# A cold beginning on one core: row numbers by iota in place of a load, two table scalings moved up, and a label for a branch hint at the end

## The chip, the cores and the metric

The kernel runs on 1 core of one Trainium2 chip. Times are microseconds of the device for one whole execution. Executions of the same program scatter by 3 to 4 us here (0.2%).

Engines: PE is the TensorE matmul engine (PEld its weight loads), DVE is VectorE, ACT is ScalarE, POOL is GpSimd, SP is SyncE, which issues most DMAs. A q behind an engine's name in a profile line (SPq, POOLq) stands for its sequencer, which waits, branches and issues DMAs.

## The reference, cut to what matters

```python
def _A_ref(x, w_r, w_i):
    X = rfft2(x.astype(float32)) * (w_r + 1j * w_i)
    return irfft2(X, s=(S, D)).astype(bfloat16)
# _B_ref: attention over 64 segments of 32 rows, 32 heads of 128, with 8 memory rows
#         that each segment hands to the next, and a projection by Wo   (cut)
x = A_x                                   # [1, 2048, 640], bf16
x = x + _A_ref(_layernorm(x), A_w_r, A_w_i)
x = x + _B_ref(_layernorm(x), B_mem0, B_Wq, B_Wk, B_Wv, B_Wo, B_seg_len)
x = x + _A_ref(_layernorm(x), A_w_r, A_w_i)
x = x + _B_ref(_layernorm(x), B_mem0, B_Wq, B_Wk, B_Wv, B_Wo, B_seg_len)
return x
```

## The kernel before

The first A layer starts cold: nothing is in SBUF yet. Row tiles of x (16 tiles of 128 rows) arrive in five loads. The layernorm is not applied to x; instead each row tile's scale is multiplied into its 128x128 Fourier table ("scaled tables"), and the mean is subtracted by extra matmuls ("means"). The stage goes in five groups of row tiles. For each group: statistics on DVE (ACT takes three of the tiles), a *small chain* that makes the scales, the scaled tables on DVE, the matmuls on PE into PSUM tiles, and the evictions of those tiles by ACT or DVE.

```python
def cold_raw(self, x_src, s3):
    ...                                                       # cut
    for a, b in ((0, 2), (2, 4), (4, 8), (8, 12), (12, 16)):
        nc.sync.dma_start(out=x[:, a:b, :], in_=r16(x_src)[:, a:b, :])
        ...                                                   # tables of a >= 4
    groups = [(0, 4), (4, 8), (8, 12), (12, 14), (14, 16)]
    pp = tc.alloc_tile_pool(name=f"{self.lname}_ps1", bufs=8, space=PSUM)   # 8 buffers, the "banks" below

    def scales(q):                                            # the small chain
        small = nc.gpsimd if q < 4 else nc.vector             # L289
        nc.scalar.activation(... func=ACTF.Ln ...)            # ACT first, L290
        nc.scalar.activation(... func=ACTF.Exp, scale=-0.5)   # L291
        ...                                                   # then seven or so ops on `small`
    def stats(t):                                             # L310, L311: bn_stats x2, bn_aggr on DVE
    def scale_tables(q):
        for t in range(*groups[q]):                           # L315
            nc.vector.tensor_scalar_mul(out=Ts[:, t, :], in0=T[:, t, :], scalar1=rs[:, t:t + 1])
    def matmuls(q):                                           # L324 rows, L329 means; five PSUM tiles
    def empties(q, ps, by):                                   # L262; one letter per PSUM tile
        ...                                                   # "A": ACT evicts it, "D": DVE
    with tc.manual_schedule(engines={PE, ACT, DVE, POOL}):    # the order below is each engine's order
        ...
        ps2 = matmuls(2)
        stats(14)
        stats(15)
        scales(4)
        empties(1, ps1, "  AAA")
        scale_tables(3)
        ps3 = matmuls(3)
        scale_tables(4)
        empties(2, ps2, "AAADD")
        empties(3, ps3, "AADAD")
        ps4 = matmuls(4)
        empties(4, ps4, "DADAD")
```

The A layer also needs rows of its weights in mirrored order. POOL gathers them with two indirect DMAs, whose row numbers 127..0 lie in a small table, itself loaded at the start by POOL's own DMA queue:

```python
def load_mirror(self, i):                                     # L220, twice in cold_raw
    nc.gpsimd.indirect_dma_start(out=self.Wm[:, i, :], in_=..., in_offset=IndirectOffsetOnAxis(ap=g["mirror"][:, 0:1], axis=0), ...)

nc.gpsimd.dma_start(out=g["mirror"][:], in_=nc.inline_tensor(np.arange(127, -1, -1, ...)).ap())   # L1595
```

The end: the last B layer adds its projection to x and stores each row tile. Then a flag decides whether a slow general version must redo the work. With this data it never does; the branch at L1676 jumps over it to the end of the program.

```python
def run(self, ...):                                           # _FastOut
    for t in range(16):
        for k in (2 * t, 2 * t + 1):
            ps = first[k] if k < len(first) else psx()
            self.accumulate(ps, k, lhs, ...)                  # 32 matmuls, L1393
            nc.vector.tensor_tensor(out=x[...], in0=ps[:, 0:320], in1=x[...], op=ALU.add)   # L1404
        if nxt is None:
            nc.sync.dma_start(out=self.xd[:, t, :], in_=x[:, t, :])                         # L1406
...
cond = nc.values_load(fa[0:1, 0:1], min_val=0, max_val=1)
with tc.If(cond > 0):                                         # L1676
    general_B(...)                                            # not taken
```

## Time and profile before

The median of 3 runs is 1582.58 us (1579.89 to 1582.95). The profiled execution took 1580.74 us by the same clock; its trace has a span of 1578.9 us, and all times of the trace below are counted in that span.

| milestone of the profiled execution | us |
|---|---|
| DVE starts statistics of row tile 4 ("row 4") | 8.57 |
| first matmul on PE | 10.88 |
| PE steps to full clock (first clock record) | 14.48 |
| first matmul of stage 2 ("S2") | 27.32 |
| first matmul of the first B layer's loop | 134.51 |
| last add starts | 1572.10 |
| SP at its branch, and its next instruction | 1573.00, 1575.55 |
| DVE at its branch, and its next instruction | 1572.73, 1575.99 |
| last output landed | 1574.71 |
| end of the span | 1578.90 |

The page of the kernel before gives the span, the busy time of each engine, and PE's busy tenths in 40 slices:

```profile
span 1578.9 us, 36639 instructions
PE 1542.9 (98%) x14420; PEld 1074.0 (68%) x14421; DVE 784.2 (50%) x2198; ACT 835.6 (53%) x2549; POOL 280.3 (18%) x327
...
PE   6999999999999999999999999999999999999998
```

Only the first slice of 39 us and the last show PE busy for less than 90%, and those are the two places that the change touches.

The timeline of the kernel before (start and duration in us, engine, line, operation, output <- inputs, count; in brackets the idle time before it and what ended it):

```profile
1.24 0.76 POOL L1595 DMA_DIRECT2D mirror<-mirror_tbl  x1 [0.78 <-POOLq L1701]
...
8.57 0.89 DVE L310 BATCH_NORM_STATS2 A1xn_S<-A1x_S 128x6 f32<-128x320 bf16 x2 [1.59 <-DMA A1x_S<-in_A_x_dram]
...
10.61 0.70 DVE L315 TENSOR_SCALAR A1xn_S<-A1xn_S 128x128 bf16<-128x128 bf16 x4
10.88 1.61 PE L324 MATMUL ps<-A1xn_S,A1x_S 128*128 128x128 bf16 x12 [10.88 <-DVE A1xn_S L311]
12.28 1.06 PE L329 MATMUL ps<-A1xn_S 128*128 128x128 bf16 x8
...
16.68 0.61 PE L329 MATMUL ps<-A1xn_S 128*128 128x128 bf16 x8
...
21.74 0.16 DVE L301 SCALAR_TENSOR_TENSOR A1xn_S<-A1xn_S 128x2 f32<-128x2 f32 x1 [0.40 <-ACT A1xn_S L291]
22.69 0.74 DVE L315 TENSOR_SCALAR A1xn_S<-A1xn_S 128x128 bf16<-128x128 bf16 x4
23.08 0.51 PE L324 MATMUL ps<-A1xn_S,A1x_S 128*128 128x128 bf16 x6 [0.21 <-DVE A1xn_S L315]
24.18 0.27 PE L324 MATMUL ps<-A1xn_S,A1x_S 128*128 128x128 bf16 x2
...
27.32 0.86 PE L424 MATMUL ab<-A1tab_S,A1YT_S 128*128 128x321 bf16 x5 [0.52 <-DVE A1YT_S L262]
```

POOL issues its small load at 1.24. DVE stood idle for 1.59 us at 8.57, until row tiles 4 to 7 of x had landed; PE's first matmul at 10.88 follows the first scaled tables, begun at 10.61. The last small chain has DVE waiting 0.40 us for ACT at 21.74, and the tables of rows 12-13 come only behind it, at 22.69; PE waits 0.21 us for them at 23.08.

Between 4 and 5 us the DMA engines are busy for 0.79 of the time and yet move only 72 GB/s: their packets are slow, not absent.

At the end, SP's own waits of the kernel before (who waited, for what: total us, times, longest):

```profile
SPq L1676 <- SPq L1676: 2.5, 1, 2.5
```

SP waits 2.5 us on itself at the branch, and the span ends 6.80 us after the last add began.

### The profile page before, as it was taken

What the parts mean: (1) busy time and instruction counts of PE and PEld (TensorE: products, weight loads), DVE (VectorE), ACT (ScalarE), POOL (GpSimd) and SP (SyncE); (2) the same over time, 40 slices, a digit from 0 to 9 for tenths busy, and PEclk for the clock granted to TensorE, in tenths of its full rate; (3) what the DMA queues carried; (4) which work ended last, traced back from release to release, by engine and by line L of the source; (5) the groups of instructions that cost most, each with busy time, mean ns of one, the idle gap of its engine ahead of it and who ended that gap; (6) DMA issues with size and microseconds to landing.
All of it is one profiled execution on the core that took longest, in us unless ns stands there. A gap on an engine that the chain in (4) does not pass through costs nothing. (4 is left out here: it accounts for less than half of the span.)

```text
span 1578.9 us, 36639 instructions
## 1 busy us (share of the span) xinstructions
PE 1542.9 (98%) x14420; PEld 1074.0 (68%) x14421; DVE 784.2 (50%) x2198; ACT 835.6 (53%) x2549; POOL 280.3 (18%) x327
## 2 busy tenths in 40 slices
PE   6999999999999999999999999999999999999998
PEld 5676666666766666677766766666766666677775
DVE  7972545455454545533377535454554545543101
ACT  4484666666666666511126656666666666663000
POOL 3620111121211112100034101111212111120000
PEclk9999999999999999999999999999999999999999
DMA  4680445445444453636114514445454454437242
GB/s 167 207 303 14 141 130 138 145 117 173 128 142 128 123 174 99 213 101 182 51 49 150 186 54 138 133 120 175 123 149 122 134 162 130 141 97 227 68 129 62
DMA packets 159922, 214.13 MB, mean 136 GB/s; under 512 B 7230, under 2 KB 133500, under 8 KB 151804
## 3 DMA queue, kind: packets, MB, share of 16 engines
q1 hardware_dynamic: 159132, 209.41, 44.7%
q8 instruction: 114, 1.87, 0.5%
q0 software_dynamic: 608, 2.30, 0.4%
q14 instruction: 68, 0.56, 0.1%
HBM read 166.59 MB, written 45.09 MB: 134 GB/s over the span
## 5 line engine op out<-in xcount | busy, mean ns | idle before, releaser
L1087 PEld LDWEIGHTS <-bB_S 128*128 128x128 bf16 x3180 | 258.0, 97 | 174.7 <-issue 1.1
L1237 DVE TENSOR_TENSOR bB_S<-pso,bB_S 128x480 bf16<-128x480 f32 (+1 forms) x320 | 189.6, 593 | 246.6 <-PE pso L1228 235.5
L1166 ACT ACTIVATE bB_S<-pss 128x269 bf16<-128x269 f32 (+5 forms) x576 | 204.1, 386 | 198.8 <-PE pss L1163 193.6
L1393 PE MATMUL psx<-Wo_sb,bB_S 128*128 128x320 bf16 x2048 | 287.7, 299 | 0.0
L1146 DVE CAST bB_S<-psk 128x495 bf16<-128x495 f32 (+3 forms) x320 | 191.8, 600 | 114.0 <-PE psk L1087 75.8
L1393 PEld LDWEIGHTS <-bB_S 128*128 128x128 bf16 x2048 | 197.1, 98 | 74.3 <-DVE bB_S L1237 0.7
L1167 DVE TENSOR_TENSOR bB_S<-bB_S,maskf 128x269 bf16<-128x269 bf16 (+5 forms) x576 | 159.6, 289 | 162.1 <-ACT bB_S L1166 162.1
L1192 POOL TENSOR_TENSOR bB_S<-bB_S,bB_S 128x634 f32<-128x634 f32 x62 | 95.1, 1534 | 682.1 <-ACT bB_S L1187 682.1
L1155 ACT CAST bB_S<-psv 128x512 bf16<-128x512 f32 (+1 forms) x288 | 161.5, 561 | 75.4 <-PE psv L1153 74.8
L1131 ACT ACTIVATE bB_S<-psq 128x96 bf16<-128x96 f32 x300 | 152.8, 509 | 91.1 <-PE psq L1087 90.2
L1153 PE MATMUL psv<-bB_S,B1hT_S 128*128 128x256 bf16 x1360 | 166.2, 273 | 0.0
L1153 PE MATMUL psv<-bB_S,B2hT_S 128*128 128x256 bf16 x1360 | 166.2, 273 | 0.0
L1087 PE MATMUL psk<-B1hT_S,bB_S 128*128 128x495 bf16 (+3 forms) x800 | 162.4, 343 | 0.4 <-ACT bB_S L1108 0.2
L1087 PE MATMUL psk<-B2hT_S,bB_S 128*128 128x495 bf16 (+3 forms) x800 | 162.4, 343 | 0.3 <-ACT bB_S L1108 0.2
L1163 PEld LDWEIGHTS <-bB_S 128*128 128x128 bf16 x1216 | 99.6, 97 | 84.4
L1087 PE MATMUL psq<-B1hT_S,bB_S 128*128 128x495 bf16 (+5 forms) x780 | 153.2, 336 | 0.0
L1087 PE MATMUL psq<-B2hT_S,bB_S 128*128 128x495 bf16 (+5 forms) x780 | 153.2, 336 | 0.0
L1153 PEld LDWEIGHTS <-B2hT_S 128*128 128x128 bf16 x1360 | 127.5, 98 | 14.6 <-issue 0.2
L1153 PEld LDWEIGHTS <-B1hT_S 128*128 128x128 bf16 x1360 | 127.5, 98 | 14.6 <-issue 0.2
L1163 PE MATMUL pss<-bB_S 128*128 128x132 bf16 (+8 forms) x1216 | 133.0, 215 | 0.1
L1228 PE MATMUL pso<-bB_S,bB_S 128*128 128x132 bf16 (+8 forms) x1216 | 120.2, 216 | 1.5 <-DVE oTmf L1238 1.4
L1228 PEld LDWEIGHTS <-bB_S 128*128 128x128 bf16 x1216 | 90.6, 98 | 22.8 <-DVE oTmf L1238 4.0
(282 smaller groups left out, 1541.8 us busy)
## 6 DMA issues: line engine op xcount, KB each, us to landing
bB_S<-Rd SPq DMA_DIRECT2D x62, 1059.5 KB
oTx_d<-bB_S SPq DMA_DIRECT2D x60, 512.0 KB
bB_S<-oTx_d SPq DMA_DIRECT2D x46, 512.0 KB
bB_S<-in_B_Wq_dram SPq DMA_DIRECT2D x32, 320.0 KB
bB_S<-in_B_Wk_dram SPq DMA_DIRECT2D x32, 320.0 KB
bB_S<-in_B_Wv_dram SPq DMA_DIRECT2D x32, 320.0 KB
Wo_sb<-in_B_Wo_dram SPq DMA_DIRECT2D x4, 1280.0 KB
B1wv_S<-in_B_Wv_dram SPq DMA_DIRECT2D x10, 512.0 KB
```

Source lines behind the costliest of these rows:

```text
L1087: nc.tensor.matmul(ps, lhsT=w[:, ch, hh * 128:(hh + 1) * 128], rhs=src[:, ch, lo:hi], start=(ch == 0), stop=(ch == 4))
L1131: nc.scalar.mul(out=qv[:, :, 0:SEG], in_=x_view(ps, o, n)[:, :, 1:SW], mul=scale)
L1146: nc.vector.tensor_copy(out=KTs[h % 2][:, lo:hi], in_=ps[:, 0:hi - lo])
L1153: nc.tensor.matmul(ps[:, i * 256:(i + 1) * 256], lhsT=hT[:, ch, st.hcol((t + i) * 128):st.hcol((t + i) * 128) + 128], rhs=w["Wv"][:, ch, : ...
L1155: nc.scalar.copy(out=V[:, t:t + n, :].rearrange("p a b -> p (a b)"), in_=ps[:, 0:n * 256])
L1163: nc.tensor.matmul(ps[:, off - o0:off - o0 + hi - lo], lhsT=KT[:, t * 128:(t + 1) * 128], rhs=QT[:, lo:hi], start=True, stop=True)
L1166: nc.scalar.activation(out=E[:, 0:n], in_=ps[:, 0:n], func=ACTF.Exp)
L1167: nc.vector.tensor_tensor(out=P[:, o0:o0 + n], in0=E[:, 0:n], in1=bs.mask[:, o0:o0 + n], op=ALU.mult)
L1192: nc.gpsimd.tensor_tensor(out=accS, in0=accS, in1=sums_sb, op=ALU.add)
L1228: nc.tensor.matmul(pso[:, lo - q0:hi - q0], lhsT=V[:, t, (h % 2) * 128:(h % 2 + 1) * 128], rhs=P[:, off:off + hi - lo], start=(i == 0), st ...
L1237: nc.vector.tensor_tensor(out=oT.rearrange("p (r s j) -> p r s j", r=16, j=2)[:, :, s0:s0 + ns, :], in0=byclass(po), in1=rx, op=ALU.mult)
L1393: self.tc.nc.tensor.matmul(ps[:, 0:320], lhsT=lhs(h, k // 2), rhs=self.g["Wo_sb"][:, h, c0:c0 + 320], start=(h == 0), stop=(h == H - 1))
```

## The change

The intent is to shorten both ends. At the cold beginning, POOL makes the row numbers itself (iota) and no longer loads them. DVE scales the tables of rows 12-13 while it would wait for ACT in the last small chain. At the end, a hint is to tell the engines about the coming branch.

```diff
@@ cold_raw
             stats(14)
             stats(15)
+            scale_tables(3)
             scales(4)
             empties(1, ps1, "  AAA")
-            scale_tables(3)
             ps3 = matmuls(3)
@@ _FastOut.run
                 ps = first[k] if k < len(first) else psx()
+                if nxt is None and k == 31:
+                    self.tc.mark_branch_hint_location("general")
                 self.accumulate(ps, k, lhs, n_first if k < len(first) else 0, H)
@@ make_globals
-    nc.gpsimd.dma_start(out=g["mirror"][:], in_=nc.inline_tensor(np.arange(127, -1, -1, dtype=np.int32).reshape(128, 1), name="mirror_tbl").ap())
+    nc.gpsimd.iota(g["mirror"][:], pattern=[[0, 1]], base=127, channel_multiplier=-1)
@@ end
-    with tc.If(cond > 0):
+    with tc.If(cond > 0, label="general"):
```

In the built programs, the instruction counts differ by one iota more and one DMA less, and nothing else. The mark emitted no hint instruction: a mark that names no engines emits none.

## The prediction

> **What bounds the kernel now.** The page has PE busy for 98% of a 1578.9 us span; only the first slice shows less (6 tenths). The change touches the first 27 us and the last 7 us.
>
> *Beginning (timeline).* PE starts at 10.88 us. The chain before it: rows 4-7 of x land, DVE statistics of row 4 start at 8.57 (1.59 us idle, ended by the DMA of x), scaled tables at 10.61, first matmul. From 8.57 to 27.3 DVE has almost no gap; stage 2 starts on PE at 27.31, released by DVE's last eviction.
>
> *End (instruction records, SP's own waits).* The last DVE add ends at 1572.59; its output lands at 1574.7. SP branches at 1573.0 and goes on only at 1575.55 (2.5 us of SP waiting on itself, with 8 and 16 KB instruction packets in that time). [...] A working hint could save at most the 0.85 us by which it outlasts the landing.
>
> **What the change does.**
>
> 1. *Iota for the load.* Removes a 0.76 us issue on POOL and a 4.4 us transfer (landed at 5.66), needed only by the mirrored gathers at 9.63 and 14.99, so its latency gates nothing. But in the packet records the first packet of rows 4-7 on each DMA engine, right behind that engine's 4-byte write of this load, takes 0.4 to 2.2 us instead of 0.196, and the data rate drops at 4.5-6 us. If the load causes that hole, rows 4-7 come up to 1 us earlier; if it is only that transfer's own start, nothing is gained. I give that one half. As built, POOL's identity memset and select (0.23, 0.29 us) move into the first small chain, which then ends near 9.6 instead of 9.06; DVE's statistics hide that. So 0 to 1.0 us, expected 0.4.
>
> 2. *Tables of rows 12-13 earlier.* Two multiplies (about 0.37 us) fill the 0.40 us in which DVE waits for ACT's exp (21.34-21.74). DVE gains 0.35 us and PE's 0.21 us wait at 23.08 goes. But the later PSUM tiles of rows 12-13 reuse banks that ACT frees until about 24.1 (PE takes the last at 24.18), and ACT's order is unchanged. So 0 to 0.2 us, about 0.1.
>
> 3. *Branch hint.* The built program has no new hint: instruction counts differ by one iota and one DMA only, and all ten prefetch hints are in the fallback's loops, as before. Gain 0.
>
> **Predicted.** About 0.5 us less: 1581.3 us, 8 in 10 between 1578.8 and 1583.2. The spread of before (1579.89 to 1582.95) exceeds the effect. Faster by over 2%: 0.005; within 2%: 0.99; slower by over 2%: 0.005.
>
> **What would show each step.** (1) DVE's statistics of row 4 move from 8.57 toward 7.6 and PE's first matmul from 10.88 toward 9.9; or both stay. (2) Table scaling ahead of the 21.7 us step, PE's idle at 23.08 gone, PE still waiting for ACT at the last tile. Stage 2 starts at 26.3 to 27.2. (3) SP's wait at the branch stays 2.5 us and the span ends 6.3 us after the last add.
>
> **What would make it wrong.** A hint that works after all (0.85 us more); an iota slow to start that delays the first small chain past 10.6 us; a table of stage 2 made late by the shifted DMAs.

## More of the kernel before

The stretches view of the kernel before (window, length, busy time and count of each engine, granted clock of PE, mean busy share of the DMA engines, GB/s). The last line is one stretch of 4 us far from the change:

```profile
core 0: us, PE busy (x) PEld busy (x) DVE busy (x) ACT busy (x) POOL busy (x), PEclk, DMA share, GB/s
4.00:5.00 1.00, 0.00 (x0) 0.00 (x0) 0.96 (x4) 0.32 (x1) 0.00 (x0) 1.00 0.79 72
5.00:6.00 1.00, 0.00 (x0) 0.00 (x0) 0.97 (x4) 0.97 (x3) 0.00 (x0) 1.00 0.71 220
72.00:76.00 4.00, 3.00 (x15) 2.08 (x15) 2.88 (x4) 1.57 (x6) 1.06 (x1) 0.57 0.67 229
```

## The result, and the profile after

The kernel after takes 1579.57 us (median of 6 runs, 1578.48 to 1581.57); before, now with 6 runs, 1580.60 us (1579.89 to 1582.95). The ratio is 0.9991 [0.9979, 1.0004]: the same within 2%, and at the edge of what can be told from no difference.

The profiled executions differ by more, 1578.9 against 1577.2 us. The page after, where every engine's busy time is nearly unchanged (PE 1541.9 against 1542.9 us):

```profile
span 1577.2 us, 36639 instructions
PE 1541.9 (98%) x14420; PEld 1073.3 (68%) x14421; DVE 783.7 (50%) x2198; ACT 834.3 (53%) x2549; POOL 279.3 (18%) x327
```

The timeline of the kernel after (its line numbers are two higher from L1402 on):

```profile
0.87 0.12 POOL L1597 IOTA mirror<- 128x1 int32 x1 [0.41 <-POOLq L1703]
...
7.69 0.89 DVE L310 BATCH_NORM_STATS2 A1xn_S<-A1x_S 128x6 f32<-128x320 bf16 x2 [0.75 <-DMA A1x_S<-in_A_x_dram]
...
10.04 1.60 PE L324 MATMUL ps<-A1xn_S,A1x_S 128*128 128x128 bf16 x12 [10.04 <-DVE A1xn_S L315]
...
20.18 0.36 DVE L315 TENSOR_SCALAR A1xn_S<-A1xn_S 128x128 bf16<-128x128 bf16 x2
20.86 0.16 DVE L301 SCALAR_TENSOR_TENSOR A1xn_S<-A1xn_S 128x2 f32<-128x2 f32 x1 [0.24 <-ACT A1xn_S L291]
21.67 0.45 PE L324 MATMUL ps<-A1xn_S,A1x_S 128*128 128x128 bf16 x4
22.33 0.27 PE L324 MATMUL ps<-A1xn_S,A1x_S 128*128 128x128 bf16 x2 [0.21 <-ACT A1YT_S L262]
...
23.30 0.27 PE L324 MATMUL ps<-A1xn_S,A1x_S 128*128 128x128 bf16 x2
...
26.44 1.82 PE L424 MATMUL ab<-A1tab_S,A1YT_S 128*128 128x321 bf16 x12 [0.52 <-DVE A1YT_S L262]
```

DVE's wait for x is 0.75 us instead of 1.59, so row 4 starts 0.88 us earlier; PE's first matmul is 0.84 us earlier (10.04) and S2 0.88 us. The iota that replaces the load took 0.12 us. From row 4 to S2 it is 18.75 us in both kernels. So the moved tables gained nothing, though they did move (20.18, ahead of the step at 20.86), and PE did begin rows 12-13 0.53 us earlier when counted from row 4 (21.67 - 7.69 = 13.98 against 23.08 - 8.57 = 14.51). PE then stands still for ACT at 22.33, which has not yet evicted a bank. The last tile of those rows starts 15.61 us after row 4 in both (23.30 - 7.69 and 24.18 - 8.57).

The stretches of the kernel after:

```profile
4.00:5.00 1.00, 0.00 (x0) 0.00 (x0) 0.97 (x4) 0.38 (x1) 0.00 (x0) 1.00 1.06 415
5.00:6.00 1.00, 0.00 (x0) 0.00 (x0) 0.96 (x4) 0.97 (x3) 0.00 (x0) 1.00 0.91 339
72.00:76.00 4.00, 3.47 (x27) 2.58 (x28) 2.75 (x5) 2.86 (x10) 0.17 (x1) 1.00 0.43 146
```

The hole at 4 to 5 us is gone: 415 GB/s against 72. SP's own wait at the branch has not changed:

```profile
SPq L1678 <- SPq L1678: 2.5, 1, 2.5
```

Where the 1.67 us between the two profiled executions (1578.90 to 1577.23) come from:

| stretch | before | after | difference |
|---|---|---|---|
| start to S2 | 27.32 | 26.44 | -0.88 |
| S2 to the first B layer's loop | 107.19 | 106.35 | -0.84 |
| loop to last add | 1437.59 | 1437.73 | +0.14 |
| last add to end | 6.80 | 6.71 | -0.09 |

The second line is not the change's. In the execution of before, PE was granted half clock for one window of 3.413 us at 72.50 (the stretch 72 to 76 above: clock 0.57, 15 matmuls started against 27); in that of after it was not (clock 1.00). Both have such a window near 847 us. In both executions PE works through the same lull there, waiting for POOL and ACT. Counted over windows of 3.413 us laid out from the clock records, PE was busy for 1.75 of the 3.41 us just before 72.50 in before, and for 1.82 and 2.13 us in the two windows that cover the lull in after. All windows of the two lulls (near 72 and 846 us) with less than 2.2 us of work, over all fourteen profiles, give the same split: the 24 with 1.13 to 1.75 us were each followed by a half-clock window, and the 7 with 1.82 to 2.16 us were not. (The boundary is no sharper than that: in e12 the window in which the kernel's work ends, with 1.74 us, was not followed by one.) And the three profiles without a half-clock window near 72 us (after, e8, e11) took 106.33 to 106.38 us from S2 to the loop, the eleven with one 107.18 to 107.82. So half of what the two traces show is this one half-clock window, and only 0.88 us are left for the change to explain, less than the scatter between executions.

### The clock in these traces

In these traces the clock changes on a grid: every half-clock window inside the work is 3.413 us long, and in before the step to full clock at 14.48 and the window at 72.50 lie 58.02 us apart, 17 windows. The other stretches of full clock in the clock records, 771.41 and 723.63 us in before and 832.85 and 723.63 us in after, are 226, 212, 244 and 212 windows long. The step has no fixed distance from the first matmul: in the eleven profiles of unwarmed kernels it came 2.86 to 5.77 us after it. This is a lottery that every comparison of single executions has to take out. It can be taken out: on the first ten profiles I fitted

S2 = the later of (row 4 + 18.72) and ((first matmul + clock step) / 2 + 14.03).

The first is DVE's chain. The second is PE's: up to the step PE does about half the work (a matmul every 107 ns, later every 56, in before), so that its 14.03 us of full-speed work ends when the formula says. It holds within 0.05 us for nine of the ten (0.12 for the tenth, e8), and it gave 26.77 for e9, which was not in the fit and measured 26.77. Before and after lie on the first branch; an execution with a late step lies on the second, and then the earlier x gains less.

### The profile page after: what moved, and what is told of

Same layout as the page of the kernel before. It is cut to its first block, busy times and chain, and to the rows that moved or that the text cites. A ratio compares the mean times of both kernels' runs of the same rounds, so it can differ in the third digit from the quotient of the medians. Undisturbed runs are those within 1.5% of the kernel's fastest.

```text
span 1577.2 us, 36639 instructions
## 1 busy us (share of the span) xinstructions
PE 1541.9 (98%) x14420; PEld 1073.3 (68%) x14421; DVE 783.7 (50%) x2198; ACT 834.3 (53%) x2549; POOL 279.3 (18%) x327
```

## The experiments

All twelve kernels gave the right result. Each timed one ran 5 times beside 9 runs of before on the same chip; e9 was a single look.

| run | what it is | median us | ratio to before [95%] | row 4 | clock step | S2 | last add to end |
|---|---|---|---|---|---|---|---|
| before | | 1580.60 | | 8.57 | 14.48 | 27.32 | 6.80 |
| after | | 1579.57 | 0.9991 [0.9979, 1.0004] | 7.69 | 13.22 | 26.44 | 6.71 |
| e1 | iota alone | 1579.87 | 0.9991 [0.9978, 1.0005] | 7.81 | 15.88 | 27.01 | 7.19 |
| e2 | tables alone | 1580.80 | 0.9998 [0.9985, 1.0012] | 8.52 | 15.30 | 27.25 | 6.66 |
| e3 | marks alone | 1581.12 | 1.0003 [0.9989, 1.0016] | 7.72 | 13.98 | 26.42 | 7.14 |
| e4 | after, plus the load, unread | 1580.48 | 0.9996 [0.9982, 1.0010] | 8.81 | 16.34 | 27.76 | 6.77 |
| e5 | real hints just before the end | 1580.87 | 1.0001 [0.9988, 1.0015] | 7.13 | 15.07 | 26.41 | 7.07 |
| e6 | real hints at the start | 1578.91 | 0.9987 [0.9974, 1.0001] | 8.39 | 15.91 | 27.37 | 4.81 |
| e7 | evictions first | 1580.49 | 0.9997 [0.9984, 1.0011] | 7.87 | 15.98 | 27.11 | 6.77 |
| e8 | the load from ACT's queue | 1580.63 | 1.0001 [0.9988, 1.0015] | 7.57 | 12.80 | 26.41 | 6.55 |
| e9 | hints in between (one run) | 1579.75 | | 8.00 | 15.19 | 26.77 | 5.86 |
| e10 | e6, PE warmed | 1577.66 | 0.9983 [0.9970, 0.9997] | 7.22 | 6.43 | 26.08 | 4.81 |
| e11 | e10, evictions first | 1577.79 | 0.9977 [0.9964, 0.9991] | 8.36 | 6.35 | 26.37 | 4.97 |
| e12 | e11, tables not moved | 1578.95 | 0.9986 [0.9973, 1.0000] | 7.98 | 5.03 | 26.71 | 4.79 |

### The three parts alone: e1, e2, e3

My theory: the load made the hole, so the iota carries all the gain; the tables and the marks carry none. The rival: the tables carry it and the hole is the transfer's own beginning.

e1 is before with the iota line alone.

```diff
-    nc.gpsimd.dma_start(out=g["mirror"][:], in_=nc.inline_tensor(...).ap())
+    nc.gpsimd.iota(g["mirror"][:], pattern=[[0, 1]], base=127, channel_multiplier=-1)
```

> Only the row numbers come from iota; table order and the end are as before. Theory (the load stalled the x packets of rows 4-7): all of the gain at the beginning is here: DVE's statistics of row 4 at 7.6 to 7.8 us (before 8.57, after 7.69), PE's first matmul near 10.0, stage 2's first matmul at 26.4 to 26.5. Rival (the earlier table scaling, not the load, made stage 2 start earlier): row 4 at 8.5, stage 2 at 27.2 to 27.4. Total about 0.9 us below before, give or take the clock windows.

Row 4 came at 7.81, very near what was expected, but S2 only at 27.01, against 26.4 to 26.5. The reason is the clock: the step came at 15.88. The timeline of e1:

```profile
27.01 1.27 PE L424 MATMUL ab<-A1tab_S,A1YT_S 128*128 128x321 bf16 x8 [0.52 <-DVE A1YT_S L262]
```

From row 4 to S2 it is 19.20 us here instead of 18.75: PE, not DVE, was the slower. This miss is what led to the formula above.

e2 is before with the tables moved alone.

```diff
+            scale_tables(3)
             scales(4)
             empties(1, ps1, "  AAA")
-            scale_tables(3)
```

> Only the tables of rows 12-13 are scaled earlier. Theory: ACT's freeing of the PSUM banks paces PE here, so PE's idle before the first matmul of rows 12-13 goes, but stage 2 starts at 27.2 to 27.35 us, at most 0.1 us earlier than before (27.32). Rival: DVE paces it, and the 0.35 us that DVE gains arrive at stage 2, near 26.97. Total within 0.2 us of before but for the clock windows.

The timeline of e2:

```profile
23.07 0.50 PE L324 MATMUL ps<-A1xn_S,A1x_S 128*128 128x128 bf16 x6
...
24.12 0.27 PE L324 MATMUL ps<-A1xn_S,A1x_S 128*128 128x128 bf16 x2
...
27.25 1.00 PE L424 MATMUL ab<-A1tab_S,A1YT_S 128*128 128x321 bf16 x6 [0.52 <-DVE A1YT_S L262]
```

PE's wait for the tables is gone from the line at 23.07, but the last tile starts at 24.12, 15.60 us after row 4, and S2 is 18.73 us after it. The tables alone are worth nothing.

e3 is before with the two lines of the hint alone.

```diff
+                if nxt is None and k == 31:
+                    self.tc.mark_branch_hint_location("general")
-    with tc.If(cond > 0):
+    with tc.If(cond > 0, label="general"):
```

> Only the mark and the label. The built program is the same as before, instruction for instruction, so this run measures what the same program scatters by. Theory: stage 2 at 27.3 plus or minus 0.1, SP idle 2.5 us after its branch, end 6.7 to 6.9 us after the start of the last add; any difference of the total from before is scatter, with a step of 0.8 to 1.0 us for each half-clock window of TensorE that one execution has and the other has not. Rival (the mark does something that the instruction list doesn't show): SP's idle falls below 1.7 us.

The built program has the same instructions as before. Its row 4 came at 7.72, as early as in the kernels without the load. Its timeline and its stretch:

```profile
7.72 0.89 DVE L310 BATCH_NORM_STATS2 A1xn_S<-A1x_S 128x6 f32<-128x320 bf16 x2 [0.61 <-DMA A1x_S<-in_A_x_dram]
```

```profile
4.00:5.00 1.00, 0.00 (x0) 0.11 (x1) 0.97 (x3) 0.23 (x1) 0.00 (x0) 1.00 0.77 90
```

The hole at 4 to 5 us is there as in before (90 GB/s), and still row 4 is early. One execution's row 4 proves nothing about the load; the packets do. Of them, more at e4. SP's wait at the branch is 2.9 us here, so the marks do nothing. S2 at 26.42, against the 27.3 expected, and the end 7.14 us after the last add, against 6.7 to 6.9, are misses: the same program scatters by more than I had allowed.

### Is it the load? e4 and e8

e4 puts the load back beside the iota, into a tile that nobody reads. If the load's traffic costs the time, it must come back.

```diff
     nc.gpsimd.iota(g["mirror"][:], pattern=[[0, 1]], base=127, channel_multiplier=-1)
+    g["mirror_d"] = sp.tile([128, 1], I32, name="mirror_d")
+    nc.gpsimd.dma_start(out=g["mirror_d"][:], in_=nc.inline_tensor(...).ap())
```

> After, with the old load put back on POOL's queue into a tile that nobody reads. Theory (the load's traffic does it): row 4's statistics go back to 8.4 to 8.6 us and stage 2 to 27.2 to 27.4, though nothing waits for the load. Rival (what counts is that the gathers no longer wait for the load, or that POOL's order changed): row 4 stays at 7.7 and stage 2 at 26.4.

Row 4 came at 8.81 and S2 at 27.76, even later than expected (S2 in part because the clock step came as late as 16.34). In the stretches of e4, the rate at 4 to 6 us is about half of what it is without the load:

```profile
4.00:5.00 1.00, 0.00 (x0) 0.00 (x0) 0.96 (x4) 0.45 (x1) 0.00 (x0) 1.00 0.91 205
5.00:6.00 1.00, 0.00 (x0) 0.00 (x0) 0.97 (x4) 0.97 (x3) 0.00 (x0) 1.00 0.63 200
```

e8 keeps the load but issues it from ACT and not from POOL, whose queue the page of before calls software_dynamic (32 packets from 3 to 7 us in before, none in after).

```diff
-    nc.gpsimd.dma_start(out=g["mirror"][:], in_=nc.inline_tensor(...).ap())
+    nc.scalar.dma_start(out=g["mirror"][:], in_=nc.inline_tensor(...).ap())
```

> Before, with the same load of 128 times 4 bytes issued from ACT in place of POOL at nearly the same time. Theory (POOL's software path stalls the DMA engines): the first 128 packets of rows 4-7 take 1 to 3 us more than 0.196 each in sum, as in the two runs without the load (1.7 and 1.4), 13 of 16 landings by 6.3 us, row 4's statistics at 7.2 to 7.8. Rival (any load of many tiny rows does it): 8 to 12 us in sum, 13 of 16 landings after 7.2.

The stretches of e8:

```profile
4.00:5.00 1.00, 0.00 (x0) 0.10 (x1) 0.58 (x2) 0.00 (x0) 0.00 (x0) 1.00 1.09 382
5.00:6.00 1.00, 0.00 (x0) 0.00 (x0) 0.97 (x4) 0.76 (x2) 0.00 (x0) 1.00 0.99 394
```

No hole. The bytes of the load are the same, but two things differ: the queue, and the time. ACT issues the load at 0.79 (POOL did at 1.24), and it has landed by 4.16, before the first packet of rows 4-7 starts at 4.60; in before it landed from 4.32 to 5.66, among those packets. So e8 does not show which of the two matters, the queue or the coincidence in time. The expectation that x would land as without the load failed, because the load now stands ahead of x: the first rows of x landed at 4.39 us instead of about 3.8. Its time, 1580.63 us, shows no gain over before.

The decisive measure is in the packet records of the trace. The first 128 packets of rows 4 to 7 have 5120 bytes each and take 0.196 us when undisturbed. What they took beyond that, summed, and the landing of the 13th and the last of the 16 DMA engines' shares of these rows:

| | sum of excess, us | 13th landing | last landing |
|---|---|---|---|
| with POOL's load: before, e2, e3, e4 | 12.4, 8.4, 9.5, 11.8 | 7.55, 7.58, 7.22, 7.27 | 8.48, 8.42, 7.62, 8.71 |
| without: after, e1, e5, e6, e7, e9, e10, e11, e12 | 1.7, 1.4, 1.0, 2.2, 2.9, 2.6, 0.8, 4.0, 4.5 | 6.15, 6.28, 6.24, 6.35, 6.33, 6.15, 6.28, 6.34, 6.39 | 7.59, 7.71, 6.37, 8.29, 7.77, 7.90, 6.41, 8.26, 7.88 |
| load from ACT: e8 | 2.4 | 6.99 | 7.09 |

The two groups do not overlap in the first two columns. In before, most slow packets are the ones right behind a 32-byte row and a 4-byte write of POOL's load (4.2 to 5.3 us; single packets of 0.99, 1.35, 1.49 and 2.17 us). The records do not name the engine; the pairing is by time: 14 packets of rows 4-7 start within 12 ns of the end of such a write, and they took 0.28 to 2.17 us. In e4 it is otherwise: 4.3 of its 11.8 us lie in packets that began before the load's first write (4.56 us), so being right behind the write is not the whole mechanism. What stretches x's packets next to the load, to as much as 2.17 us, is not in the records.

The last column shows why row 4 scatters all the same. DVE starts right behind the last share (landed at 8.48, start 8.57 us in before; 7.59 and 7.69 in after), and in seven of the nine profiles without POOL's load the last landed 1.43 to 1.94 us behind the 13th, in the other two 0.13. The packet records here do not name the engine, so the cause of these late shares stays open. Over all profiles, row 4 starts at 8.41 us on average with POOL's load (four) and at 7.83 without (nine): 0.58 us. But the two groups overlap (7.72 to 8.81 and 7.13 to 8.39), so for row 4 itself the difference is likely and not proven; it is the packets that the load changes without overlap.

### The hint: e5, e6, e9

With `engines=` given, a mark emits real hint instructions. e5 puts them behind the last work of row tile 14: 3 instructions ahead of the branch on SP, 4 on DVE, and about 138 on PE, counted in the trace.

```diff
+                if t == 14:
+                    for ins, e in ((mm, nc.tensor), (add, nc.vector), (dma, nc.sync)):
+                        with self.tc.issue_after(ins.ins):
+                            self.tc.mark_branch_hint_location("general", engines=[e.engine])
```

> After, with the mark made to emit: engines are named (PE, DVE, SP), and each hint stands behind that engine's work for row 14, some 5 to 8 us before the end. Theory (the 2.5 to 3 us after the branch are a fetch that a real hint can start earlier): SP's idle after its branch falls from 2.5-3.0 us to below 1.7 us and is then ended by the landing of the last output; span end minus start of the last add falls from 6.7-7.2 us to 5.7-6.2. Rival (the idle is the wait for the output's landing, or the fetch starts only at the branch): both stay. Beginning as in after: excess of the first 128 packets of rows 4-7 below 3 us.

For SP and DVE that theory failed. SP's own wait in e5, and likewise DVE's 3.3 us from branch to next instruction, stayed:

```profile
SPq L1681 <- SPq L1681: 2.7, 1, 2.7
```

PE's hint worked, which does not show at the end because PE is done before the others: its branch instruction took 0.41 us, against 3.35 to 3.77 us in the nine profiles where PE has no hint, after among them, and a 16 KB instruction packet starts 1.2 us behind the hint (1561.86 and 1560.63), where after has none. DVE's and SP's hints were as early in time, 9.3 and 8.7 us ahead of their branches. So it is not the time that they lacked.

e6 takes the change's own mark and only adds the engines. The built program then has the hint as the first instruction of all five engines, since nothing ties it to a place.

```diff
-                    self.tc.mark_branch_hint_location("general")
+                    self.tc.mark_branch_hint_location("general", engines=list(mybir.ALL_ENGINES))
```

> After, with the changed kernel's own mark at its own place, and all five engines named. The build puts the five hints at the very start of the program, whole milliseconds of instructions ahead of the branch. Theory A (a hint is held until its branch): same end as with the late hints. Theory B (it only fetches at once[...]): end as in after, 6.7 to 7.2 us behind the start of the last add; up to 0.3 us later start.

SP went on 0.53 us after its branch and DVE 0.61 us (2.55 and 3.26 in before). SP's own waits in e6:

```profile
SPq L1678 <- SPq L1678: 0.9, 2, 0.5
```

The span ended 4.81 us after the last add instead of 6.80; over all profiles it is 4.79 to 4.97 us with hints at the start (four) and 6.55 to 7.19 with no hint or hints just before the end (nine). Neither of the two theories had this: late hints and hints at the start do not end alike, and the early hint's effect was not gone after 1570 us. In the timed runs, e6 is at a mean of 1578.90 us beside 1580.85 for its before.

e9 separates distance from presence: SP's hint some 490 instructions before its branch, DVE's 47 before.

```diff
+                        with tc.issue_after(dma.ins):           # SP, in the first B layer
+                            tc.mark_branch_hint_location("general", engines=[nc.sync.engine])
+            if nxt is None and t == 0:                          # DVE, in the last B layer's output loop
+                with self.tc.issue_after(add.ins):
+                    self.tc.mark_branch_hint_location("general", engines=[nc.vector.engine])
```

> After, with hints on two engines alone at two distances: SP's some 490 of its instructions ahead of its branch (behind a load at the end of the first B layer), DVE's 47 ahead (behind the first add of the last stage). The hints 3 and 4 instructions ahead did nothing, those at the program's start did. Theory [...]: SP's idle after the branch is below 0.7 us as with hints at the start, DVE's stays at 3.2 to 3.4 us. Rival (only a hint at the head of the program works): both stay (SP 2.5 to 3.1). Second rival (3 or 4 instructions were just too few): both fall. Span end minus start of the last add: between 4.8 and 7.1, set by the slower engine.

SP's branch took 0.53 us and DVE's 3.27 us, in one and the same execution. SP's waits of e9, none of which at the branch is longer than 0.7 us:

```profile
SPq L1681 <- SPq L1681: 1.2, 2, 0.7
...
SPq L1720 <- DVEq L1681: 1.0, 1, 1.0
```

The second line is the point: once SP's branch is quick, SP waits 1.0 us for DVE at the end. Both engines must be hinted; e9's tail of 5.86 us lies between 6.80 and 4.81. A hint worked 494 instructions ahead of its branch (SP) and about 138 (PE in e5), and not 47, 4 or 3 ahead (DVE in e9, DVE and SP in e5). But these are different engines and the exact limit was not tried, so the least distance, and why the distance counts, stay open. e9's single run has an unknown state; its reading rests on the waits of two engines in the same execution, not on its time.

### Why the moved tables gave nothing: e7, e10, e11, e12

The reading of after was that ACT frees the banks too late. ACT's order has the last small chain's two operations ahead of the evictions of rows 4-7's tiles. e7 turns that around.

```diff
+            empties(1, ps1, "  AAA")
             scale_tables(3)
             scales(4)
-            empties(1, ps1, "  AAA")
             ps3 = matmuls(3)
```

> After, with ACT's three evictions of rows 4-7's last tiles ahead of the last small chain, in the 1.2 us in which ACT waits for DVE there. Theory (ACT's freeing of PSUM banks paces PE in rows 12-15): row 4's statistics to stage 2 takes 18.2 to 18.4 us in place of 18.70 to 18.75, and PE no longer waits inside rows 12-13. Rival (PE's work or DVE's evictions pace it): 18.65 to 18.8. A late step of TensorE to full clock (after 15 us) can add 0.4 us to either.

Inconclusive: the clock step came at 15.98, PE was busy without a gap from 17.3 to 26.6 us, and S2 was 19.24 us after row 4 as the second branch of the formula has it. Nothing that helps DVE or ACT can show while PE is behind. So the clock had to be taken out. e10 is e6 with 84 matmuls on data that is there early, written to a PSUM tile that nobody reads, so that PE's clock step comes before the work.

```diff
+            warm = pp.tile([128, 4, 128], FP32, name="warm", tag="pa")
+            for n, w in ((32, g["ones"][:]), (28, x[:, 2, 0:128]), (24, x[:, 4, 0:128])):
+                for i in range(n):
+                    nc.tensor.matmul(warm[:, i % 4, :], lhsT=w, rhs=g["ones"][:], start=True, stop=True)
             act_stats(3)
```

> After, with hints on all engines at the program's start and 84 matmuls of no use on PE before the first real one (their result is never read), so that TensorE's step to full clock comes early. From ten profiles: stage 2 starts at the later of row 4's statistics + 18.72 us and half of (PE's first real matmul + step) + 14.03 us, within 0.1. Theory (that law): the step comes before 9.5 us, and stage 2 starts 18.65 to 18.85 us after row 4's statistics. Rival (the extra 0.3 to 0.5 us of four runs had another cause): 18.9 to 19.3. End 4.7 to 5.0 us behind the start of the last add. Total 0 to 0.5 us below the run with the hints at the start (1578.91).

The timeline of e10:

```profile
1.24 3.59 PE L347 MATMUL warm<-ones 128*128 128x128 bf16 x32 [1.24 <-DVE ones L1608]
...
10.78 0.61 PE L329 MATMUL ps<-A1xn_S 128*128 128x128 bf16 x8
...
22.12 0.27 PE L324 MATMUL ps<-A1xn_S,A1x_S 128*128 128x128 bf16 x2 [0.21 <-ACT A1YT_S L262]
...
26.08 2.10 PE L428 MATMUL ab<-A1tab_S,A1YT_S 128*128 128x321 bf16 x14 [0.52 <-DVE A1YT_S L262]
```

The first real means-matmuls take 0.61 us already, the clock step is at 6.43, and PE still waits for ACT at 22.12, with S2 18.86 us after row 4. That is a hair above the 18.65 to 18.85 expected, and below the rival's 18.9 to 19.3. The hair has a likely reason: row 4 came so early (7.22) that DVE's first tables (9.44) start right behind POOL's last multiplication of the scales (9.21 to 9.41), 2.22 us after row 4 against 2.04 in before. By this trace an x that lands earlier still would gain little, though no run tried it. A warm PE alone does not shorten DVE's chain; it only removes the late branch. The median, 1577.66 us, is 1.25 us below e6's, more than the 0 to 0.5 expected, but on another chip. e11 adds e7's order.

```diff
+            empties(1, ps1, "  AAA")
             scale_tables(3)
             scales(4)
-            empties(1, ps1, "  AAA")
```

> The run before, with ACT's three evictions of rows 4-7 ahead of the last small chain; the earlier run of that edit fell in an execution in which PE stepped up late and set the pace, which told nothing. Theory (with PE at full clock early, ACT's freeing of the PSUM banks paces PE in rows 12-15): stage 2 18.2 to 18.45 us after row 4's statistics. Rival (DVE's or PE's own work is the limit all the same): 18.65 to 18.85.

The timeline of e11:

```profile
8.36 0.89 DVE L310 BATCH_NORM_STATS2 A1xn_S<-A1x_S 128x6 f32<-128x320 bf16 x2 [1.20 <-DMA A1x_S<-in_A_x_dram]
...
26.37 1.82 PE L428 MATMUL ab<-A1tab_S,A1YT_S 128*128 128x321 bf16 x12 [0.52 <-DVE A1YT_S L262]
```

S2 comes 18.01 us after row 4, 0.74 less than before and after, a larger gain than expected (18.2 to 18.45). Row 4 itself was late here (8.36), from a late last share (landed at 8.26, the 13th at 6.34). e12 takes the moved tables away again from e11.

```diff
             empties(1, ps1, "  AAA")
-            scale_tables(3)
             scales(4)
+            scale_tables(3)
```

> The run before (hints at the start, early full clock, ACT's three evictions first), with the tables of rows 12-13 scaled after the last small chain again, as the kernel before had it: the change's second step taken back where ACT and PE's clock no longer cover it. Theory (the step is worth something only once ACT frees the banks in time): PE's first matmul of rows 12-13 waits 0.4 to 0.7 us for DVE, and stage 2 starts 18.3 to 18.65 us after row 4's statistics in place of 18.01. Rival (it is worth nothing here either): 17.9 to 18.15.

The timeline of e12:

```profile
7.98 0.89 DVE L310 BATCH_NORM_STATS2 A1xn_S<-A1x_S 128x6 f32<-128x320 bf16 x2 [0.74 <-DMA A1x_S<-in_A_x_dram]
...
22.67 0.51 PE L324 MATMUL ps<-A1xn_S,A1x_S 128*128 128x128 bf16 x6 [0.70 <-DVE A1xn_S L315]
...
26.71 1.55 PE L428 MATMUL ab<-A1tab_S,A1YT_S 128*128 128x321 bf16 x10 [0.52 <-DVE A1YT_S L262]
```

Now PE waits 0.70 us for the tables, and S2 is 18.73 us after row 4 (slightly outside the 18.3 to 18.65 expected). So with PE warm: tables moved only, 18.86; evictions first only, 18.73; both, 18.01. (Counted from PE's first real matmul, which leaves out e10's wait for POOL: 16.33, 16.38 and 15.71, against 16.44 in before, with neither.) The two waits of PE, for DVE's tables and for ACT's banks, lie side by side, and taking away either one leaves the other to end the wait. The change took away one.

e11 beats both kernels: its mean is 1577.51 us beside 1580.80 for before on the same chip, a ratio of 0.9977 [0.9964, 0.9991]. That is 3.3 us, of which the hint's tail is about 2.0 (e6's trace). The gains do not simply add up: in e11 and e12 the stretch from the first loop to the last add took 1438.85 and 1439.15 us, 1.1 us or more above before and after (1437.59 and 1437.73), and no run asks why.

## Why the prediction was right

It said 1581.3 us with a range of 1578.8 to 1583.2, within 2%; the median measured is 1579.57, in the range. That alone says little: the range is 4.4 us wide and holds "no change" as well, and before's own median fell from 1582.58 to 1580.60 us between its first 3 runs and all 6. The gain was 1.0 us by the medians and 0.88 us in the profiled beginning, against 0.5 predicted. What speaks for the prediction is the steps. Point by point:

1. **The load.** The prediction gave even chances to the hole being the load's doing, and put 0 to 1.0 us on it, 0.4 expected. It is the load's doing: the packet excess falls from 8.4-12.4 us (four profiles) to 0.8-4.5 us (nine), without overlap, and returns when the load returns (e4). With the same load issued earlier through ACT's queue it stays away too (2.4, e8), at the price of later first rows; whether the queue or the earlier time spares rows 4-7 is not shown. The prediction's picture, the packet right behind each 4-byte write, fits before and not all of e4. In the profiled pair row 4 gained 0.88 us and S2 the same, near the top of the range. Over executions it is less, because a late last share often sets the landing anyway: 0.58 us in the mean of row 4. The timed runs say the same: the 42 runs of before have a mean of 1580.9 us, and the 21 runs of kernels without the load and without a working hint (after, e1, e5, e7) one of 1580.3, some 0.6 us less. The 15 runs of kernels that keep the load (e2, e3, e4) have a mean of 1580.8, like before. These are averages over several chips, and the differences are within the scatter of single runs, so they support the size and do not prove it.
2. **The tables.** Expected 0.1 us, measured 0.00 (18.75 us from row 4 to S2 in both, and 18.73 in e2). The reason that the prediction gave, ACT's unchanged order, is the one shown: PE's wait moved to ACT's eviction at 22.33, and with ACT's order turned around and PE warm the same two multiplies are worth 0.72 us (18.73 of e12 against 18.01 of e11).
3. **The hint.** Expected 0, as no hint instruction was built. SP's wait stayed 2.5 us and the span ended 6.22 us after the end of the last add, as against 6.31. The side remark that a working hint "could save at most the 0.85 us" by which SP's wait outlasts the output's landing was mis-sized: hints at the start cut the tail from 6.80 to 4.81 us, 2.0 us. By the semaphore records, SP does not look at the landing as soon as it goes on. In before it first passes seven other semaphores and comes to the output's at 1576.08, 1.37 us after the landing (1574.71); in e6 it has passed them by the time the output lands (1575.41) and goes on at 1575.43. Counted from the start of the last add, this point comes 1.68 us earlier (2.31 instead of 3.99), 0.32 us of it because the output itself landed earlier. The other 0.32 us lie behind that point, and no run shows their cause. DVE's wait at its branch has to go too. In before it costs nothing, since DVE goes on at 1575.99 and SP comes to it later, but with SP's hint and not DVE's (e9) SP waits 1.0 us for DVE and the tail is only 0.94 us shorter.

What the prediction did not see was the clock. Where the clock step falls decides whether PE or DVE is late at S2 (up to 0.5 us in e1, e5 and e7), and a half-clock window falls at 73 us in one execution and not in another (0.84 us between the profiled pair). The prediction named the spread of before as larger than the effect, which was enough for a range, but not why.

Left open: why the last share of x often lands late without the load; how POOL's load stretches the packets next to it, and whether its queue or its time does it; and the least distance at which a hint works.

## What to carry to other kernels

A tiny load from GpSimd's queue landed here long before it was needed (5.66 against 9.63 us) and still went with slow packets in a large load on the critical path that ran at the same time (8.4 to 12.4 us of excess with it, 0.8 to 4.5 without): look at the data rate right behind it, and make the values on the chip if they can be computed (the iota took 0.12 us). Where two engines feed a third, look for the wait that would end next before moving one of them; it took ACT's order and DVE's order together to gain anything. Check in the built program that a hint became an instruction, and how many instructions ahead of its branch it stands, and read single executions only after the phase of the PE clock has been taken out.
